# Sigmoid attention followed by a SiLU feed-forward on one core: batch 1's attention moved into the first matmul of batch 0, and the second matmul evened out to two pairs per batch

## Chip, cores, metric

One core of one Trainium2 chip. The metric is the device time of one execution in microseconds (us), median of several runs. The profiled span is 1.7 to 2.9 us shorter than that time, mostly 1.8, and all positions below are times from the start of the span.

Engine names: PE is the matrix engine (PEld its weight loads), DVE the vector engine, ACT the scalar engine with the sigmoids, POOL (GpSimd) casts and issues one DMA queue, SP issues the other.

## The reference

```python
# q, k, v: (8, 12, 448, 64), normal * 0.1
scores = q @ k.T / sqrt(64) - log(448)
attn   = sigmoid(scores)                # no softmax, so no row maximum and no row sum
x      = (attn @ v) -> (8*448, 768)
h      = x @ w_in                       # 768 -> 2048, "ff1" below
out    = (h * sigmoid(h)) @ w_out       # 2048 -> 768, "ff2" below
```

## The kernel before

Everything runs in float16 with float32 accumulation. A batch has 448 tokens. Its 12 heads are taken in three groups of four: groups 0, 1, 2 are batch 0, groups 3, 4, 5 are batch 1. The parts that matter:

```python
# loads: two queues
def load16(kind, i): ... nc.gpsimd.dma_start(...)        # POOL queue, casts to f16 on the way
def load32(kind, i): ... nc.sync.dma_start(st32[2 * (i % 2) + kind] ...)   # SP queue, stays f32
def cast(kind, i):   nc.gpsimd.tensor_copy(st16[i % 3][kind], st32[...])   # POOL
def dma_transpose(kind, i): nc.sync.dma_start_transpose(qkT[i % 3][kind], st16[i % 3][kind])
def pe_transpose(kind, i, pair): ...     # the same on PE with an identity, DVE copies PSUM to qkT

# attention: one score step = 4 small matmuls, then one sigmoid of 128x896 on ACT
def score_step(i, r, pair): ...          # needs qkT of group i
def value_steps(i, pair, rs): ...
def to_x(i, pair): ...                   # evicts attention output to xT

# [...]
dummy(14)                                # matmuls on zeros, to warm up PE
pe_transpose(1, 0, 0)
pe_transpose(0, 0, 1)
for n in range(NQ):                      # batch 0: 21 score steps, PE transposes of groups 1, 2 between
    for r in range(R):
        score_step(n, r, cnt % 2); sigmoid(n, r, cnt % 2)
        # [...] transposes, value_steps, or dummy(2)

for b in range(B):
    lo, hi = (b * S) // 256, ((b + 1) * S) // 256     # pairs of row blocks that batch b completes
    ff1(b, early)                        # 96 matmuls of 448 columns
    # ff2 of pairs lo..hi-1 (56 matmuls of 384 columns each, a Strassen-like form)
    # interleaved with the attention of batch b + 1
```

A pair is 256 tokens and a batch has 448, so batches 0 and 4 get one pair and the other six get two. q and k of the groups from 3 on come by SP as f32, are cast by POOL and transposed by DMA into qkT, the transposed q and k that the scores read; v comes by the POOL queue. The schedule rests on each engine taking its instructions in the order of the program. All four w_in pieces are queued in the opening, w_out right behind.

## Time and profile before

405.4 us (three runs, 404.7 to 405.8); the profiled execution took 406.5 us, with a span of 404.3 us. The total hides the structure, so I cut the span where each ff1 starts.

| stage (from ff1 of batch b to the next) | pairs of ff2 | us |
|---|---|---|
| start: attention of batch 0 | – | 34.4 |
| 0 | 1 | 49.8 |
| 1, 2, 3 | 2 each | 47.4 each |
| 4 | 1 | 40.4 |
| 5, 6 | 2 each | 47.3, 47.1 |
| 7 (no attention beside it) | 2 | 43.0 |

These come from the timeline of PE. A line gives start, length, engine, source line, operation, output<-inputs, form and count, and in brackets the idle time before it with what ended it. The 36-matmul runs are the halves of an ff1; those at 84.22, 131.66 and so on are the first halves:

```profile
63.91 0.59 PE L140 MATMUL att<-qkT,qkT 64*64 64x448 f16 x4 [7.20 <-DMA qkT<-st]
84.22 6.97 PE L215 MATMUL att<-xT,w_in_sb 128*128 128x448 f16 x36
131.66 6.97 PE L215 MATMUL att<-xT,w_in_sb 128*128 128x448 f16 x36
226.55 6.97 PE L215 MATMUL att<-xT,w_in_sb 128*128 128x448 f16 x36
266.92 6.97 PE L215 MATMUL att<-xT,w_in_sb 128*128 128x448 f16 x36
```

From 226.55 to 266.92 is stage 4. The line at 63.91 is a score of group 4 that waited 7.20 us for its DMA transpose; this happened behind ff1 of batch 0, in stage 0.

The busy time of the engines in three stretches (columns: stretch, length, then busy time and count of PE, PEld, DVE, ACT, POOL, then the granted PE clock, DMA share, GB/s): ff2 of stage 4, ff2 of a two-pair stage, and the score steps of batch 0:

```profile
244.00:266.90 22.90, 20.69 (x224) 10.03 (x223) 10.72 (x16) 19.52 (x23) 5.40 (x8) 1.00 0.57 102
286.00:314.00 28.00, 27.65 (x267) 13.90 (x266) 16.01 (x25) 19.46 (x21) 5.12 (x7) 1.00 0.55 111
8.00:34.40 26.40, 22.58 (x286) 9.55 (x286) 9.39 (x15) 19.45 (x21) 14.26 (x21) 1.00 1.23 209
```

In the two-pair stretch PE is busy 27.65 of 28.00 us: that stage is PE-bound. In the one-pair stretch PE has 20.69 of 22.90 and ACT 19.52: the 2 us of slack is what one-pair stages waste. The score steps of batch 0 run with the DMA engines at a share of 1.23 (above 1, so packets that overlap are counted more than once): busy throughout.

The score steps of batch 0, each four matmuls, with a dummy pair between (timeline of PE), and SP's queue, which shows when transposes are issued:

```profile
11.32 0.38 PE L140 MATMUL att<-qkT,qkT 64*64 64x448 f16 x4 [1.92 <-DVE qkT L127]
12.14 0.38 PE L140 MATMUL att<-qkT,qkT 64*64 64x448 f16 x4
12.46 0.61 PE L81 MATMUL ffp<-warm 128*128 128x512 f16 x2
```

```profile
28.24 2.76 SPq L110 DMA_TRANSPOSE qkT<-st  x2
31.06 5.98 SPq L101 DMA_DIRECT2D st<-in_k_dram  x2
53.48 6.26 SPq L110 DMA_TRANSPOSE qkT<-st  x2
```

A score step takes 0.38 us. Transposes of group 3 are issued at 28.24 and of group 4 at 53.48; the first score that needs group 3 comes at 50.8.

### The profile page before, as it was taken

The numbers are of one execution on the slowest core, as the hardware profiler recorded it, in microseconds if no ns is written. First come the engines' busy times: TensorE is split into PE (matmuls) and PEld (weight loads), VectorE is DVE, ScalarE is ACT, GpSimd is POOL, SyncE is SP. The second block draws the span as 40 slices with busy tenths as digits, with TensorE's granted clock in tenths as the row PEclk, the third lists the DMA queues.
The fourth block names the chain that finished last, engine by engine and source line by source line (L and its number), as shares of the span: only waits on it lengthen the run. The fifth ranks groups of instructions, "written<-read, shape, count | busy, mean of one in ns | idle before, by whom it ended". The sixth has DMA issues, their size and how long they took to land.

```text
span 404.3 us, 7303 instructions
## 1 busy us (share of the span) xinstructions
PE 378.2 (94%) x3026; PEld 188.3 (47%) x3026; DVE 201.6 (50%) x281; ACT 219.1 (54%) x251; POOL 81.5 (20%) x114
## 2 busy tenths in 40 slices
PE   6889956899999999999999998899999999999994
PEld 2334522455445545555455554455455544455452
DVE  1341545744646455544546354445645455544662
ACT  1885372924874348734677239933874348734200
POOL 7561034221222130022112022302112000000000
PEclk9999996999999999999999999999999999999999
DMA  8999987879977772767547783778178630311022
GB/s 194 199 206 200 208 151 155 161 156 214 161 150 159 180 148 47 175 133 178 107 72 188 175 172 71 155 162 163 39 143 164 170 47 2 78 42 40 0 78 78
DMA packets 69472, 53.78 MB, mean 133 GB/s; under 512 B 42304, under 2 KB 65856, under 8 KB 69440
## 3 DMA queue, kind: packets, MB, share of 16 engines
q1 hardware_dynamic: 55840, 40.38, 43.9%
q0 software_dynamic: 13600, 12.95, 21.8%
q8 instruction: 23, 0.38, 0.4%
q14 instruction: 9, 0.07, 0.1%
HBM read 45.61 MB, written 11.01 MB: 140 GB/s over the span
## 4 chain that ended last, share of the span: by engine, by line
PE 75%; DMA 12%; ACT 3%; POOL 3%; SPq 3%; issue 2%; DVE 1%; POOLq 0%; ACTq 0%
PE ffp L267 31%; PE att L215 24%; PE ffp L215 7%; PE att L156 7%; DMA st<-in_q_dram 7%; PE att L140 6%; DMA w_in_sb<-in_moe_w_in_dram 3%; ACT attnT L146 2%; SPq L101 2%; POOL st L104 1%; DMA st<-in_k_dram 1%; DMA qkT<-st 1%; ACT tsig L226 1%; SPq L110 1%; DVE gT L228 1%
## 5 line engine op out<-in xcount | busy, mean ns | idle before, releaser
L146 ACT ACTIVATE attnT<-att,bias_s 128x896 f16<-128x896 f32 x168 | 156.9, 1012 | 47.4 <-PE att L140 46.7
L215 PE MATMUL att<-xT,w_in_sb 128*128 128x448 f16 x576 | 111.8, 352 | 0.2 <-ACT xT L168 0.2
L215 PEld LDWEIGHTS <-w_in_sb 128*128 128x128 f16 x768 | 74.9, 98 | 70.6 <-issue 1.4
L230 ACT ACTIVATE tsig<-att 128x896 f16<-128x896 f32 x48 | 44.0, 917 | 99.6 <-PE att L215 99.6
L231 DVE TENSOR_TENSOR gT<-att,tsig 128x896 f16<-128x896 f32 x48 | 52.4, 1092 | 75.6 <-ACT tsig L230 75.6
L104 POOL CAST st<-st 128x896 f16<-128x896 f32 x42 | 40.7, 971 | 195.0 <-DMA st<-in_k_dram 153.4
L140 PE MATMUL att<-qkT,qkT 64*64 64x448 f16 x672 | 49.2, 360 | 12.5 <-DMA qkT<-st 8.0
L267 PEld LDWEIGHTS <-gs 128*128 128x128 f16 x448 | 40.0, 98 | 40.7 <-issue 12.0
L267 PE MATMUL ffp<-w_out_sb,gT 128*128 128x384 f16 x224 | 43.7, 328 | 3.4 <-DVE gT L228 3.4
L267 PEld LDWEIGHTS <-gT 128*128 128x128 f16 x336 | 31.1, 98 | 30.0 <-issue 11.6
L170 DVE TENSOR_SCALAR xT<-att 128x896 f16<-128x896 f32 x23 | 25.1, 1091 | 39.1 <-PE att L156 39.1
L267 PE MATMUL ffp<-wt,gs 128*128 128x384 f16 x224 | 42.5, 331 | 0.5 <-DVE gs L289 0.5
L267 PE MATMUL ffp<-w_out_sb,gs 128*128 128x384 f16 x224 | 42.4, 327 | 0.0
L215 PE MATMUL ffp<-xT,w_in_sb 128*128 128x448 f16 x192 | 39.0, 353 | 0.0
L278 DVE TENSOR_SCALAR snap<-ffp 128x384 f32<-128x384 f32 x42 | 23.4, 557 | 28.6 <-PE ffp L267 26.1
L156 PE MATMUL att<-attnT,v 64*64 64x448 f16 x672 | 37.5, 359 | 0.0
L97 POOL DMA_DIRECT2D v<-in_v_dram x48 | 28.6, 601 | 41.7 <-PE att L140 35.4
L140 PEld LDWEIGHTS <-qkT 64*64 64x64 f16 x672 | 17.8, 105 | 40.0 <-issue 32.4
L281 DVE SCALAR_TENSOR_TENSOR osb<-ffp,snap 128x384 f32<-128x384 f32 x42 | 23.3, 554 | 20.3 <-PE ffp L267 19.6
L156 PEld LDWEIGHTS <-v 64*64 64x64 f16 x672 | 18.4, 108 | 17.1 <-issue 8.8
L226 ACT ACTIVATE tsig<-ffp 128x448 f16<-128x448 f32 x32 | 17.2, 546 | 11.3 <-PE ffp L215 11.3
L228 DVE TENSOR_TENSOR gT<-ffp,tsig 128x448 f16<-128x448 f32 x32 | 19.7, 620 | 6.1 <-ACT tsig L226 6.1
(31 smaller groups left out, 126.4 us busy)
## 6 DMA issues: line engine op xcount, KB each, us to landing
out_dram<-osb SPq DMA_DIRECT2D x56, 192.0 KB, 2.8
st<-in_k_dram SPq DMA_DIRECT2D x44, 224.0 KB, 4.3
st<-in_q_dram SPq DMA_DIRECT2D x42, 224.0 KB, 4.9
v<-in_v_dram POOLq DMA_DIRECT2D x48, 112.0 KB, 4.1
w_in_sb<-in_moe_w_in_dram POOLq DMA_DIRECT2D x4, 768.0 KB, 10.9
w_out_sb<-in_moe_w_out_dram POOLq DMA_DIRECT2D x4, 768.0 KB, 22.8
st<-in_q_dram POOLq DMA_DIRECT2D x6, 112.0 KB, 7.5
qkT<-st SPq DMA_TRANSPOSE x42, 3.5
```

Of the source, the lines that this page charges most:

```text
L97: nc.gpsimd.dma_start(o[g * HP : (g + 1) * HP], src_of(kind, i, g))
L104: nc.gpsimd.tensor_copy(st16[i % 3][kind].rearrange("p r e d -> p e r d"), st32[2 * (i % 2) + kind].rearrange("p e (r d) -> p e r d", r=R),)
L140: nc.tensor.matmul(att[pair][cj, e, :S], kT[re, r, cj], qT[re, :, cj], start=True, stop=True)
L146: nc.scalar.activation(attnT[:, s0 : s0 + 2, :], att[pair][:, :, :S], AF.Sigmoid, bias=bias_s, scale=QKSCALE)
L156: nc.tensor.matmul(att[pair][e * HP : (e + 1) * HP, j, :S], vt[rj, e, r, :], attnT[rj, s0 + e, :], start=(r == 0), stop=(r == R - 1),)
L170: nc.vector.tensor_scalar_mul(xT[:, 2 * n : 2 * n + 2, :], att[pair][:, :, :S], SX)
L215: nc.tensor.matmul(o, w_in_sb[:, cc, f * P : (f + 1) * P], xT[:, cc, :], start=(cc == 0), stop=(cc == NCC - 1),)
L228: nc.vector.tensor_mul(gT[:, 2 * u + e, cb : cb + S], ffp[e][:, :S], ts[:, e])
L230: nc.scalar.activation(ts, ph[:, :, :S], AF.Sigmoid, bias=0.0, scale=ISX)
L231: nc.vector.tensor_mul(gT[:, 2 * u : 2 * u + 2, cb : cb + S], ph[:, :, :S], ts)
L267: nc.tensor.matmul(bank, a[:, fc], w[:, fc], start=first and fc == 0, stop=fc == KH - 1, skip_group_check=True,)
L278: nc.vector.tensor_scalar_mul(snap[i], bank, ISX)
```

## The change

Intent: no more one-pair stages. Attention of batch 1 runs inside ff1 of batch 0, where PE alone was busy and ACT idle; ff2 then runs two pairs per batch, one batch behind, for batches 1 to 7. The transposes in batch 0 are cut into halves and used as fillers between scores. Two w_in pieces and w_out are issued later, so that group 3 can come earlier. Two tiny memsets ("gates") keep SP from fetching groups 3 and 4 too early.

The core of the diff (definitions of the halved transposes and of ff1 as a generator cut):

```diff
-    xT = sb("xT", [P, NCC, S])
+    xT = [sb(f"xT{i}", [P, NCC, S]) for i in range(2)]
 [...]
     w_in_piece(1)
-    load16(2, 2)
-    w_in_piece(2)
-    w_in_piece(3)
-
-    dummy(14)
-    pe_transpose(1, 0, 0)
-    pe_transpose(0, 0, 1)
+    dummy(10)
+    for half in range(2):
+        pe_transpose(0, 0, 1, half, dve)
+    for half in range(2):
+        pe_transpose(1, 0, 0, half, act)
+    ff0 = ff1(0, (3, 2))
 [...]
+        (1, 0): [lambda: gate(3), lambda: fetch(3), T(1, 2, 0)],
 [...]
+        (1, 3): [T(0, 2, 1), lambda: prepare(3), lambda: w_in_piece(2)],
 [...]
+        (2, 0): [V(0, 6), X(0), lambda: gate(4), lambda: fetch(4)],
+        (2, 3): [V(1, 2, 3, 4), lambda: prepare(4), lambda: w_in_piece(3)],
+        (2, 6): [V(2, 0, 1, 2, 3), F("part", 0), V(2, 4, 5), F("part", 1)],
 [...]
+    us = units_of(1)                       # attention of batch 1, two steps at a time
+    visit(vs.pop(0))
+    for x in ff0:                          # between the column blocks of ff1 of batch 0
+        if vs and x[0] == "end" and x[1] % 4 != 1:
+            visit(vs.pop(0))
+    for s in range(4):
+        w_out_piece(s)
-    for b in range(B):
-        lo, hi = (b * S) // 256, ((b + 1) * S) // 256
+    for b in range(1, B):
 [...]
-            for m in range(lo, hi):
+            for m in (2 * b - 2, 2 * b - 1):
                 yield from ff2_pair(m)
```

`prepare(i)` is cast and DMA transpose of k and q of group i; `fetch(i)` is their loads and that of v.

## The prediction

> What bounds the kernel now. The page gives a span of 404.3 us, PE busy 94%; the chain of waits is 75% PE, 12% DMA. By stage (timeline of PE): batch 0's attention takes 34.4 us, paced by ACT (21 sigmoids of about 0.93 us) and by loads. Then each batch has ff1 (96 matmuls, 18.2 us) and ff2 mixed with the next attention. Stages with two ff2 pairs take 47.2 to 47.4 us and are PE-bound. Those with one pair are not: stage 4 takes 40.4 us (ACT sigmoids in its chain), stage 0 takes 49.8 us (8.0 us of PE waiting for DMA transposes, plus the one-time weight sums on DVE, eight of 0.95 to 1.68 us). The last stage takes 42.8 us. In the first 65 us the DMA is full.
>
> What the change does. Fourteen ff2 pairs remain, now two in each of batches 1 to 7. Batch 1's attention moves into ff1 of batch 0. Dummy matmuls become useful fillers. w_in pieces 2 and 3 move behind the casts of groups 3 and 4, w_out behind those of group 7.
>
> Cost. Before: 34.4 + 49.8 + 3x47.4 + 40.4 + 47.4 + 47.2 + 42.8. After: start + A + stage 1 + 5x47.2 + 42.8, where A is ff1 of batch 0 with attention of batch 1.
> Start: copies split over ACT and DVE save about 1 us, finer fillers about 1: 33 us.
> A: ACT needs 21x1.0 + 8 = 29 us, PE about 26, so ACT bounds it; plus 3.5 us for the last value product and its eviction: 33 us when data is there. It may not be: load, cast and transpose of one group recur every 10 us even without other traffic (transposes issued at 67.3, 77.1), and transposes beside weight loads are slow (issued 28.2, landed after 45). I expect about 6 us of waits for groups 4 and 5: A 39 us.
> Stage 1: 47 us plus about 4 for the weight sums, which load DVE beyond PE in the first pair. From the trace's rates (a weight piece 4 us, a group with transposes 10 us) all DMA work up to w_out's end adds to 95 to 98 us; the third product wants it at about 97. So little extra wait, but no slack: anything won earlier is lost there.
> Total: 33 + 39 + 51 + 236 + 43 = 402 us; without DMA waits 395 to 396. I say 400.5, range 393.5 to 408; chances: faster by over 2% 0.25, within 2% 0.70, slower 0.05.
>
> The Trainium skill ("DMA: Bandwidth & Descriptors", Queues, rings and completion order) says that each DMA engine goes round the queues packet by packet. The trace agrees: while w_out moved in 1536-byte packets, two transposes in 256-byte packets took about 15 us instead of 5.
>
> What would show it. Timeline: ff1 of batch 1 starting at about 72 us (not before 65), stages 2 to 6 at 47.2 us each including stage 4, last stage unchanged. In A, ACT nearly full except for waits of PE score matmuls for qkT of groups 4 and 5. In stage 1, DVE weight sums waiting for w_out or nearly, PE stalls of about 4 us in the first pair.
>
> What would make it wrong. Transposes landing in time: about 396. w_out landing past 100 us, or the clock falling to half in a PE stall as before at 55 to 61 us: 405 to 410. Score steps stalling behind k and q of group 2 in the start, because group 3's loads now compete earlier.

## The result, and the profile after

412.3 us (four runs, 410.6 to 412.8), against 405.6 us for the kernel before in four runs. Ratios in this document are the mean time of one kernel's runs over that of the other's of the same rounds, so not quite the ratio of the medians: here 1.0159, with an interval of 1.0122 to 1.0195. The change made the kernel 1.6% slower. That is within the 2% either way to which I had given a chance of 0.70, but above my range of 393.5 to 408 us.

The same lines of the timeline of PE for the changed kernel:

```profile
39.72 0.57 PE L137 MATMUL att<-qkT,qkT 64*64 64x448 f16 x8 [2.08 <-DMA qkT<-st]
54.50 0.59 PE L137 MATMUL att<-qkT,qkT 64*64 64x448 f16 x4 [6.64 <-DMA qkT<-st]
82.78 6.97 PE L217 MATMUL att<-xT,w_in_sb 128*128 128x448 f16 x36 [1.74 <-DVE xT L168]
131.66 6.97 PE L217 MATMUL att<-xT,w_in_sb 128*128 128x448 f16 x36
225.80 6.97 PE L217 MATMUL att<-xT,w_in_sb 128*128 128x448 f16 x36
272.86 6.97 PE L217 MATMUL att<-xT,w_in_sb 128*128 128x448 f16 x36
```

Read it by stages. "Stage A" is ff1 of batch 0 with the attention of batch 1; it begins with the first score of batch 1, at 39.72.

| | before | predicted | after |
|---|---|---|---|
| start (to the first score of batch 1) | – | 33 | 39.7 |
| stage A | – | 39 | 43.1 |
| sum: start of ff1 of batch 1 | 84.2 | 72 | 82.8 |
| stage 1 | 47.4 | 51 | 48.9 |
| stage 4 | 40.4 | 47.2 | 47.1 |
| stages 2, 3, 5, 6 | 189.3 | 188.8 | 188.4 |
| last stage | 43.0 | 42.8 | 43.1 |
| span | 404.3 | 402 | 410.2 |

So one ff2 pair left stage 0, and that brought ff1 of batch 1 forward by only 1.4 us. The pair was then paid for elsewhere: stage 4 grew by 6.7 us, the one-time weight sums moved into stage 1 (1.4 us). The deficit, 5.9 us, is the sum of these (-1.4 + 1.4 + 6.7) less the 0.9 us that stages 2, 3, 5 and 6 gained, plus 0.1 in the last. The later stages came out as predicted. The loss is in the first 83 us, where I was wrong by 10.8 us.

The score steps in the opening, SP's queue, and two stretches of busy time (5 us of the opening, and stage A):

```profile
11.31 0.59 PE L137 MATMUL att<-qkT,qkT 64*64 64x448 f16 x4 [0.57 <-ACT qkT L126]
12.39 0.59 PE L137 MATMUL att<-qkT,qkT 64*64 64x448 f16 x4
14.23 1.04 PE L81 MATMUL ffp<-warm 128*128 128x512 f16 x2
22.80 0.38 PE L137 MATMUL att<-qkT,qkT 64*64 64x448 f16 x4
27.54 0.64 PE L137 MATMUL att<-qkT,qkT 64*64 64x448 f16 x4
```

```profile
28.29 3.98 SPq L110 DMA_TRANSPOSE qkT<-st  x2
32.35 2.47 SPq L101 DMA_DIRECT2D st<-in_k_dram  x2
43.76 3.74 SPq L110 DMA_TRANSPOSE qkT<-st  x2
```

```profile
10.00:15.00 5.00, 3.95 (x34) 1.75 (x33) 1.25 (x2) 3.30 (x5) 1.71 (x3) 1.00 1.10 162
39.70:82.80 43.10, 32.38 (x257) 13.04 (x257) 12.08 (x15) 26.77 (x33) 13.67 (x18) 0.88 0.84 159
```

Three things are to be seen.

First, a score step takes 0.59 us until 22 us, then 0.38, and 0.64 again from 26.4 to 28.7 us. A dummy pair takes 1.04 instead of 0.61. By these lengths PE runs at about half clock for the first half of batch 0. The Trainium skill ("TensorE: Matmul & The Clock Gate", Part 1: The HAM clock gate) says that PE starts at half clock, and that a window of about 3.4 us of sustained work releases it. The traces agree only in part. The longer opening of the kernel before (14 dummies, 5.23 us) was followed by full-speed scores and the shorter one (10 dummies, 4.45 us) was not. But the number of dummies does not settle it: in runs 2, 4 and 14 below, also with 10, the eight transpose matmuls right behind them took 0.41 us, the full-speed length (0.64 here). In runs 2 and 4 the scores were at 0.59 us again from 10.5 and 11.7 us on; in run 14 they stayed at 0.38 until 19 us. The transposes of the opening, between which PE waits 0.8 and 0.7 us here, may count as well. Run 1 adds dummies in both places, so no run parts the two. Note that the stretch from 10 to 15 us shows a clock of 1.00 all the same; the matmul lengths are to be trusted there, not that column.

Second, the DMA transposes of group 3 are issued at 28.29, as late as in the kernel before (28.24), but now their scores come right behind: PE waits until 39.72. Group 4's are issued at 43.76 and land only by 54.50.

Third, ACT, which I had expected to be nearly full in stage A, is busy 26.77 of 43.10 us.

### The profile page after: what moved, and what is told of

The parts are those of the page before. It is cut to its first block, busy times and chain, and to the rows that moved or that the text cites. A ratio compares the mean times of both kernels' runs of the same rounds, so it can differ in the third digit from the quotient of the medians.

```text
span 410.2 us, 7255 instructions
## 1 busy us (share of the span) xinstructions
PE 382.4 (93%) x3000; PEld 188.6 (46%) x3000; DVE 198.5 (48%) x285; ACT 221.7 (54%) x255; POOL 81.4 (20%) x114
## 4 chain that ended last, share of the span: by engine, by line
PE 83%; DVE 5%; DMA 4%; ACT 4%; issue 2%; SPq 0%; POOL 0%; ACTq 0%; POOLq 0%
PE ffp L275 30%; PE att L217 25%; PE ffp L217 9%; PE att L137 8%; PE att L153 7%; DMA st<-in_q_dram 2%; ACT attnT L143 2%; DMA qkT<-st 2%; PE ffp L81 2%; PE att L119 1%; DVE qkT L126 1%; ACT tsig L233 1%; DVE gs L297 1%; DVE xT L168 1%; DVE wt L253 1%
## 5 line engine op out<-in xcount | busy, mean ns | idle before, releaser
L143 ACT ACTIVATE attnT<-att,bias_s 128x896 f16<-128x896 f32 x168 | 158.6, 1008 | 49.1 <-PE att L137 48.3
L217 PE MATMUL att<-xT,w_in_sb 128*128 128x448 f16 x552 | 109.2, 355 | 1.7 <-DVE xT L168 1.7
L237 ACT ACTIVATE tsig<-att 128x896 f16<-128x896 f32 x46 | 42.2, 917 | 92.7 <-PE att L217 92.7
L238 DVE TENSOR_TENSOR gT<-att,tsig 128x896 f16<-128x896 f32 x46 | 50.2, 1092 | 75.3 <-ACT tsig L237 75.3
L137 PE MATMUL att<-qkT,qkT 64*64 64x448 f16 x672 | 52.6, 379 | 12.2 <-DMA qkT<-st 8.7
L217 PE MATMUL ffp<-xT,w_in_sb 128*128 128x448 f16 x216 | 46.9, 364 | 0.0
L275 PE MATMUL ffp<-w_out_sb,gT 128*128 128x384 f16 x224 | 43.1, 327 | 0.4 <-DVE gT L235 0.4
L153 PE MATMUL att<-attnT,v 64*64 64x448 f16 x672 | 39.1, 360 | 0.3 <-DVE qkT L126 0.3
L137 PEld LDWEIGHTS <-qkT 64*64 64x64 f16 x672 | 18.7, 108 | 40.4 <-issue 33.9
L235 DVE TENSOR_TENSOR gT<-ffp,tsig 128x448 f16<-128x448 f32 x36 | 22.0, 620 | 26.1 <-ACT tsig L233 26.1
L233 ACT ACTIVATE tsig<-ffp 128x448 f16<-128x448 f32 x36 | 19.2, 548 | 11.3 <-PE ffp L217 11.3
```

What stands on the lines that cost most here:

```text
L137: nc.tensor.matmul(att[pair][cj, e, :S], kT[re, r, cj], qT[re, :, cj], start=True, stop=True)
L143: nc.scalar.activation(attnT[:, s0 : s0 + 2, :], att[pair][:, :, :S], AF.Sigmoid, bias=bias_s, scale=QKSCALE)
L153: nc.tensor.matmul(att[pair][e * HP : (e + 1) * HP, j, :S], vt[rj, e, r, :], attnT[rj, s0 + e, :], start=(r == 0), stop=(r == R - 1),)
L217: nc.tensor.matmul(o, w_in_sb[:, cc, f * P : (f + 1) * P], x[:, cc, :], start=(cc == 0), stop=(cc == NCC - 1), skip_group_check=split,)
L233: nc.scalar.activation(ts[:, e], ffp[e][:, :S], AF.Sigmoid, bias=0.0, scale=ISX)
L237: nc.scalar.activation(ts, att[pr][:, :, :S], AF.Sigmoid, bias=0.0, scale=ISX)
```

## The experiments

The theories:

- C: the cold clock costs the start.
- D: the start is bound by group 3's transposes, and the clock does not matter.
- G: the gates hold group 3 back.
- W: transposes are late because a w_in piece, issued right behind the casts, runs beside them.
- P: the chain load, cast, transpose is itself too slow, or DMA as a whole is full; then moving the weights only moves the wait.

Seventeen kernels ran, each timed beside the kernel before. In the table, "start" is the first score of batch 1, "waits" the waits of PE for qkT of groups 3, 4, 5, "ff1(1)" the start of ff1 of batch 1, all from the timeline of PE; the last columns are the median and the ratio to the kernel before.

| run | start | waits 3 / 4 / 5 | ff1(1) | us | ratio |
|---|---|---|---|---|---|
| changed kernel | 39.7 | 2.1 / 6.6 / 0 | 82.8 | 412.3 | 1.0159 |
| 1 warm | 36.4 | 3.2 / 5.8 / 0 | 79.5 | 410.0 | 1.0097 |
| 2 w_in early | 43.3 | 6.8 / 3.1 / 0 | 81.4 | 411.2 | 1.0111 |
| 3 warm and w_in early | 42.0 | 7.5 / 2.4 / 0 | 80.4 | 409.8 | 1.0099 |
| 4 no gates | 38.4 | 0 / 4.5 / 0 | 77.7 | 408.0 | 1.0045 |
| 5 warm, no gates | 37.7 | 3.2 / 5.8 / 0 | 79.3 | 408.6 | 1.0061 |
| 6 fourth w_in piece later | 37.4 | 3.9 / 2.7 / 4.4 | 80.7 | 409.8 | 1.0099 |
| 8 kernel before, 10 dummies | – | – | 86.9 | 407.5 | 1.0030 |
| 10 stale q, k (wrong) | 33.3 | 0 / 0 / 0 | 69.3 | 400.0 | 0.9814 |
| 11 half of w_in (wrong) | 34.6 | 0 / 3.6 / 0 | 72.8 | 401.2 | 0.9848 |
| 13 groups 3, 4 transposed on PE | 38.0 | 0 / 0 / 0 | 76.1 | 408.2 | 1.0064 |
| 14 the same, 10 dummies | 41.4 | 0 / 0 / 0 | 79.5 | 412.7 | 1.0157 |
| 15 ff1 first | 38.7 | 5.1 / 0.8 / 2.7 | 77.6 | 408.0 | 1.0047 |
| 16 ff1 first, w_in one group later | 34.3 | 0 / 0 / 4.7 | 76.4 | 407.4 | 1.0048 |
| 17 w_in one group later | 33.8 | 0 / 6.6 / 0 | 76.3 | 407.2 | 1.0007 |

Runs 7, 9 and 12 had mistakes of mine and are told below. The intervals of the ratios are about 0.005 to each side. Start, waits and ff1(1) are those of one profiled execution each. Nothing in which runs 5, 6 and 15 differ takes place before the first score of group 3, and yet they waited 3.2, 3.9 and 5.1 us there and started at 37.7, 37.4 and 38.7: differences of 1 to 2 us between single executions mean nothing.

### Runs 1 to 4: clock, weights, gates

Run 1, warm:

```diff
-    dummy(10)
+    dummy(14)
     for half in range(2):
         pe_transpose(0, 0, 1, half, dve)
+        dummy(2)
     for half in range(2):
         pe_transpose(1, 0, 0, half, act)
+        dummy(2)
```

> The changed kernel with 14 instead of 10 opening dummy matmuls and two more between each half of the opening transposes. Theory C (the start lost to a cold TensorE clock: four-matmul score steps of 0.59 us instead of 0.38 until 22 us): the score steps of batch 0 run at 0.38 us from the first on, the 21st sigmoid ends about 3 us earlier (about 33 us instead of 35.7), the load gate falls near 15.5 instead of 18.2 us, so group 3's transposes land about 2.5 us earlier and the total falls by 2 to 4 us, to 408 to 410 us. Rival D (the start is lost to the late transposes of group 3 alone): batch 0 ends earlier but PE waits longer for qkT, batch 1 still starts at 39.7 us, total unchanged at 412.

Timeline of PE in run 1:

```profile
12.01 0.38 PE L137 MATMUL att<-qkT,qkT 64*64 64x448 f16 x4
13.15 0.38 PE L137 MATMUL att<-qkT,qkT 64*64 64x448 f16 x4
36.38 0.96 PE L137 MATMUL att<-qkT,qkT 64*64 64x448 f16 x8 [3.20 <-DMA qkT<-st]
79.52 6.97 PE L217 MATMUL att<-xT,w_in_sb 128*128 128x448 f16 x36 [1.74 <-DVE xT L168]
```

The score steps are at 0.38 us, and ff1 of batch 1 starts 3.3 us earlier. The ratio falls from 1.0159 to 1.0097 (the two intervals overlap a little). C is right that the clock has a part, but D has one too: the sigmoids of batch 0 now end at 31.2 instead of 35.7, 4.5 us earlier, and PE stands 3.2 us for group 3. The gate memset sits in DVE's queue behind copies that wait for PE, so a warm PE also opens it earlier (at 16.4 instead of 18.2 us): group 3's transposes are issued at 24.3 instead of 28.3.

Run 2, all w_in pieces in the opening, as before:

```diff
+    w_in_piece(1)
     load16(2, 2)
-    w_in_piece(1)
+    w_in_piece(2)
+    w_in_piece(3)
 [...]
-        (1, 3): [T(0, 2, 1), lambda: prepare(3), lambda: w_in_piece(2)],
+        (1, 3): [T(0, 2, 1), lambda: prepare(3)],
-        (2, 3): [V(1, 2, 3, 4), lambda: prepare(4), lambda: w_in_piece(3)],
+        (2, 3): [V(1, 2, 3, 4), lambda: prepare(4)],
```

> The changed kernel with all four w_in pieces issued in the prologue, as the kernel before has it. Theory W (w_in pieces 2 and 3, issued right after the casts, run beside the transposes of groups 3 and 4 and delay them): transposes of group 3 take about 5 us from issue instead of 9 to 11, group 4 likewise, the 6.6 us wait shrinks to under 3 us, total 405 to 408 us. Rival P (the load, cast, transpose chain itself has a period of about 10 us, whatever the weights do): group 3's loads now land about 8 us later behind the weights, the start of batch 1 moves to 42 us or later, total unchanged or worse, 411 to 416.

Group 3 came 3.6 us later (start 43.3), group 4's wait halved to 3.1; total 411.2. The wait moved from group 4 to group 3, as P says. This run does not refute W: the pieces now ran beside group 3's loads and transposes.

Run 3, both edits:

> Both edits. If the two losses are independent the gains add (404 to 407 us). If the clock only moves the wait (D) it equals the early w_in alone; if the weights only displace the loads (P) it equals the warm one alone.

The result, 409.8, can be told neither from run 1 (410.0) nor, within noise, from run 2 (411.2); only the added gains of 404 to 407 us are ruled out. With the weights early, the warm opening changed the start by only 1.3 us: group 3 set it, with waits of 6.8 and 7.5 us.

Run 4, no gates: the two `gate(...)` calls are dropped.

> The changed kernel without the two memsets that hold back the fetches of groups 3 and 4. If the gate holds group 3 back too long (its k arrives at 27 us, the casts then wait 7.5 us for it), loads of group 3 land about 5 us earlier, its transposes by 33 us, and the total falls by 2 to 5 us. If instead early loads take bandwidth from groups 0 to 2, the first scores start later than 11.3 us and the total is the same or up to 3 us worse.

Group 3's transposes were issued at 21.0 us and landed at about 35.0 (39.6 in the changed kernel), before batch 0 was done, so its wait vanished; 408.0, ratio 1.0045. The score steps took 0.59 to 0.64 us here until 29 us, and yet this was better than run 1. G is right that the gates opened too late.

### Runs 5 to 8: combining, and two dead ends

Run 5, warm and no gates:

> The warm opening and no gates together. Alone they gave about 2 and 4 us. In the warm run batch 0 ended at 31.2 us and PE then waited 3.2 us for group 3; without the gates group 3 was there in time. If the clock and the gate are the two causes of the late start, batch 1 now starts at about 33 us without a wait. But group 4 landed at 50.3 us without gates, bound by DMA: then the wait for it grows from 4.5 to about 8 us and the total stays near 407. If group 4 follows group 3 forward, 404 us.

SP's queue and the timeline of PE:

```profile
20.79 2.95 SPq L110 DMA_TRANSPOSE qkT<-st  x2
37.68 0.57 PE L137 MATMUL att<-qkT,qkT 64*64 64x448 f16 x8 [3.16 <-DMA qkT<-st]
```

No gain on run 4 (408.6). Batch 0 was done early, but group 3, with transposes issued at 20.8, landed only for the score at 37.7: 17 us. Issuing them 7.5 us earlier than in the changed kernel brought them in only 2 us earlier. So what holds group 3 is mostly not when its transposes are issued; the next runs ask what runs beside them.

Run 6 adds, to run 5, the fourth w_in piece behind the casts of group 5 instead of group 4:

> As the last, and the fourth w_in piece moves from behind the casts of group 4 to behind those of group 5. Theory W (transposes of group 4 are slow because that piece runs beside them): they take 5 to 6 us from issue instead of about 10, the wait for group 4 falls by 4 to 5 us, total 402 to 404 us. Rival P (the chain itself is the limit): wait unchanged, total as the last or worse because the fourth piece arrives late for ff1.

Group 4's wait fell from 5.8 to 2.7 as W says, and group 5, which had none, got one of 4.4; total 409.8. The wait followed the weight piece.

Run 7 was meant to transpose groups 3 and 4 on PE:

> The changed kernel, warm, with groups 3 and 4 loaded and cast by the queue of GpSimd like groups 1 and 2 and transposed on TensorE (as batch 0 is), so that they need neither the cast nor the DMA transpose; group 5 is fetched early. If the chain load, cast, DMA transpose is what keeps batch 1 back, both waits of PE for qkT vanish, batch 1 starts at about 33 us, ff1 of batch 1 at 67 to 70 us, and the total is 395 to 399 us, below the kernel before. If stage A is slow for a reason of its own (PE and ACT alternating in order), it stays at 40 us or more and the total is 401 or above.

It gave a wrong result (relative error 0.2672) and 441.5 us. The loads of group 3 came ahead, in program order, of the opening transposes of group 0 that read the same buffer; PE waited 15.6 us for them. The wrong result itself has another source: run 9, without this mistake, shows the same error of 0.2672, from a misplaced load of v that run 7 has too. Nothing follows about the theories.

Run 8, the kernel before with `dummy(10)`:

> The kernel before with 10 instead of 14 opening dummy matmuls. If the number of dummies decides the clock in the start, its score steps take 0.59 us for some 10 us. There the start is also limited by ACT and by the loads, and group 3 is not needed until 51 us, so the total rises by at most 2 us, to 406 to 408; no change at all if the clock still comes up in time.

Its first scores take 0.59 us and ff1 of batch 1 comes at 86.9 instead of 84.2 us in the profiled run. In time it is 407.5, ratio 1.003 (0.998 to 1.008): within noise. The same cold opening costs the old order little that can be shown, since group 3 is not needed until 51 us.

### Runs 9 to 12: taking the waits away

Run 9, a second try at the PE transposes:

> The seventh run mended (there the loads of group 3 came ahead of the opening transposes in the program, so that those read group 3's rows): same idea, the loads of groups 3 and 4 now follow the transposes that free their buffers. Expectation as before: if the chain load, cast, DMA transpose keeps batch 1 back, no wait of PE for qkT of groups 3 and 4, batch 1 starts at about 33 us, stage A takes about 35 us, ff1 of batch 1 starts at 67 to 70 us, total 395 to 399 us. If stage A is slow for its own reason, 401 or above.

Wrong again, 430.0 us: v of group 5 was loaded, in program order, ahead of the value steps of group 1 that still read its buffer (PE waited 16.8 us).

Run 10: the warm kernel without cast and transpose of groups 3 to 5.

```diff
-        (1, 3): [T(0, 2, 1), lambda: prepare(3), lambda: w_in_piece(2)],
+        (1, 3): [T(0, 2, 1), lambda: w_in_piece(2)],
-        (2, 3): [V(1, 2, 3, 4), lambda: prepare(4), lambda: w_in_piece(3)],
+        (2, 3): [V(1, 2, 3, 4), lambda: w_in_piece(3)],
 [...]
-        at(("s", i, 3), lambda j=i + 2: prepare(j))
+        if i > NQ:
+            at(("s", i, 3), lambda j=i + 2: prepare(j))
```

> Wrong on purpose: the warm kernel without casts and DMA transposes of groups 3 to 5, so that the scores of batch 1 use the transposes of batch 0 and never wait for any. It shows start and stage A without that wait: batch 1 starts at about 32.5 us; stage A takes 33 us if ACT bounds it as predicted (29 us of ACT work and the end), or 36 to 37 us if the wait-free rest of stage A in the trace (43 less 6.6) is of another cause. Total 394 to 398 us.

Busy time of its stage A (same columns as above) and the start of ff1 of batch 1:

```profile
33.30:69.30 36.00, 30.46 (x260) 12.71 (x253) 12.70 (x16) 26.97 (x34) 10.23 (x14) 0.95 1.02 192
```

```profile
69.34 6.97 PE L217 MATMUL att<-xT,w_in_sb 128*128 128x448 f16 x36 [1.74 <-DVE xT L168]
```

400.0 us, ratio 0.9814. Without waits the start takes 33.3 us, as predicted, and stage A 36.0 instead of the 33 I had counted. ACT is still busy only 26.97 us of it: the waits of ACT for scores fall from 14.3 us in the changed kernel to 5.4, and the last 3.4 us of the stage are the last value product and its eviction. I put this down to PE and ACT taking turns in a fixed order, so that neither fills; no run changed that order with the waits gone. (With q and k of size 0.1 the sigmoid hardly depends on them, so the correctness check is blind to q and k. For every run here, the changed kernel too, "correct" does not vouch for q and k; only the order of the program does.)

Run 11: the warm kernel without w_in pieces 2 and 3.

```diff
-                            w_in_sb[:, cc, f * P : (f + 1) * P],
+                            w_in_sb[:, cc, f % 8 * P : (f % 8 + 1) * P],
```

> Wrong on purpose: the warm kernel without w_in pieces 2 and 3 (ff1 uses the first two pieces twice), so transposes of groups 3 and 4 run with no weight load beside them. Theory W: group 3 lands about 5 us after issue (by 30 us), no wait at the start of batch 1, wait for group 4 under 2 us, total 399 to 402. Rival P (the chain of load, cast, transpose, or loads slowed by other loads): the waits shrink by less than half, total 406 or above.

Timeline of PE and SP's queue:

```profile
45.30 0.38 PE L137 MATMUL att<-qkT,qkT 64*64 64x448 f16 x4 [3.58 <-DMA qkT<-st]
72.77 6.97 PE L217 MATMUL att<-xT,w_in_sb 128*128 128x448 f16 x36 [1.74 <-DVE xT L168]
```

```profile
27.69 3.76 SPq L110 DMA_TRANSPOSE qkT<-st  x2
37.92 3.28 SPq L110 DMA_TRANSPOSE qkT<-st  x2
47.72 3.23 SPq L110 DMA_TRANSPOSE qkT<-st  x2
```

401.2 us, and the wait for group 3 is gone although its transposes were issued 3.4 us later than in run 1. The later transpose of group 3 landed at most 4.3 us after its issue and that of group 4 after 5.2, against 9.1 and 8.0 in run 1. So two w_in pieces beside the transposes are most of the waits, which fall from 9.0 to 3.6 us in all (W). Group 4 still waited 3.6 us: transposes recur every 10 us even with no weight piece beside them, which is P, and I had expected less than 2.

Run 12, third try at the PE transposes:

> The ninth run mended: there v of group 5 was fetched, in program order, ahead of the value products of group 1 that still read its buffer, so PE waited 16.8 us for it and used the wrong v. Now it follows them. Expected: correct; no wait of PE for qkT of groups 3 and 4 since TensorE transposes them; batch 1 starts at 33 to 34 us; stage A takes 36 to 38 us, as the stale-scores run showed 36.0 us without any wait; ff1 of batch 1 starts at 70 to 72 us; total 398 to 402 us, faster than both kernels. If the loads of groups 3 and 4 or w_in pieces come too late because DMA itself is full, PE waits for them instead and the total is 404 or above.

425.0 us. Now the DMA transposes of group 5 came, in program order, ahead of the last scores of group 2 in the same buffer, and PE waited 18.6 us. Runs 7, 9 and 12 taught one lesson three times: in this kernel the order of the program, not the order in time, decides what waits for what.

### Runs 13 and 14: transposes on PE, warm and cold

The valid version of that idea. Groups 3 and 4 come by the casting queue and are transposed by PE, so that they need neither POOL's cast nor a DMA transpose:

```diff
+    load16(1, 3); load16(0, 3); w_in_piece(1); load16(2, 3)      # behind the opening transposes
 [...]
-        (0, 4): [T(0, 1, 1)],
+        (0, 4): [T(0, 1, 1), load16(1, 4), load16(0, 4), w_in_piece(2)],
+        (2, 1): [T(1, 3, 0), T(1, 3, 1)],
+        (2, 5): [T(0, 3, 0), T(0, 3, 1)],
 [...]                                   # group 4's in stage A; group 5 fetched from (2, 0) on
```

> The twelfth run mended: there the DMA transposes of group 5 came, in program order, ahead of the last two scores of group 2, whose buffer they overwrite, so PE waited 18.6 us for them. Now they follow batch 0. Expected if late transposes are the cause of the loss: no wait of PE for groups 3 and 4, batch 1 starts at 33 to 34 us, stage A takes 36 to 38 us, ff1 of batch 1 starts at 70 to 72 us, total 398 to 402 us. If the loads only move the wait elsewhere (DMA full), the total is 404 or above.

Timeline of PE around the inserted transposes of group 3:

```profile
30.02 0.38 PE L137 MATMUL att<-qkT,qkT 64*64 64x448 f16 x4
31.18 0.41 PE L119 MATMUL att<-ident,st 128*64 128x128 f16 x8 [0.78 <-DMA st<-in_q_dram]
32.38 0.36 PE L119 MATMUL att<-ident,st 128*64 128x128 f16 x6 [0.78 <-DVE qkT L126]
32.67 0.56 PE L137 MATMUL att<-qkT,qkT 64*64 64x448 f16 x4
```

No wait for qkT remains, and yet the start is at 38.0 and stage A takes 38.1; 408.2 us. From one score to the next took 2.65 us here instead of the usual 0.9: PE waits for the loads and for DVE's copies of what it has transposed. The waits were turned into round trips, and behind them PE ran at half clock for a while: the 16 value matmuls at 33.4 us took 1.71 us, 0.95 in run 1. My estimate of 398 to 402 was wrong.

Run 14 gives that kernel the cold opening:

> The same kernel with the changed kernel's opening (10 dummies, none between the opening transposes). It shows what the clock alone costs when no DMA transpose of group 3 stands behind it: if the cold clock costs time of its own, batch 1 starts 3 to 4 us later than in the run beside it and the total is 2 to 4 us higher; if the clock only mattered through the load gate, no difference beyond 1 us.

Timeline of PE in run 14:

```profile
9.93 0.38 PE L137 MATMUL att<-qkT,qkT 64*64 64x448 f16 x4 [0.57 <-ACT qkT L126]
18.01 0.41 PE L119 MATMUL att<-ident,st 128*64 128x128 f16 x8 [1.54 <-DMA st<-in_k_dram]
19.66 0.59 PE L137 MATMUL att<-qkT,qkT 64*64 64x448 f16 x4
```

412.7 against 408.2 us, ratios 1.0157 and 1.0064 with intervals of 0.004: the shorter opening costs about 4 us where no DMA transpose of group 3 stands behind it. It is not the clean test of a cold start that it was meant to be. In the profiled execution (410.2 us, the fastest of six) the scores begin at full length, and PE falls to half clock only at 19 us, behind a wait of 1.5 us for k of group 2; the granted clock from 20 to 25 us is 0.50, and 1.00 in run 13. The other five executions, of 411.4 to 413.6 us, left no trace. So a lower clock goes with the loss, but how much of the 4 us it makes is not shown. Beside runs 4 and 5, where the opening made no difference, this fits C and D together: the opening counts as far as group 3 is there in time.

### Runs 15 to 17: order of ff1, place of w_in

Run 15, on run 5: four column blocks of ff1 in a row ahead of group 4's first score.

```diff
-        if vs and x[0] == "end" and x[1] % 4 != 1:
+        if vs and x[0] == "end" and not 2 <= x[1] <= 5:
```

> The warm kernel without gates, with the attention steps of batch 1 moved within ff1 of batch 0: four column blocks of ff1 in a row ahead of the first score of group 4, where PE waited 5.8 us. If the in-order PE queue makes the wait for group 4 cost its full length although ff1 could have run, the wait falls to about 1 us, and since ACT still has its sigmoids left to do, stage A shrinks by about 3 us; total 404 to 406 us. If ACT bounds the rest anyway, total unchanged at 408.

Group 4's wait fell to 0.8, but group 5 now waited 2.7; 408.0, the same as run 5 within noise.

Run 16 has that order too, and each late w_in piece one group later, with the gate and fetch of group 3 at the second score of batch 0 and no gate for group 4:

```diff
-        (0, 1): [T(1, 1, 1)],
+        (0, 1): [T(1, 1, 1), lambda: gate(3), lambda: fetch(3)],
-        (1, 3): [T(0, 2, 1), lambda: prepare(3), lambda: w_in_piece(2)],
+        (1, 3): [T(0, 2, 1), lambda: prepare(3)],
-        (2, 3): [V(1, 2, 3, 4), lambda: prepare(4), lambda: w_in_piece(3)],
+        (2, 3): [V(1, 2, 3, 4), lambda: prepare(4), lambda: w_in_piece(2)],
 [...]                                   # w_in_piece(3) behind prepare(5)
```

> That order of steps, and each late w_in piece one group later (third behind the casts of group 4, fourth behind those of group 5), with group 3 fetched from the second score of batch 0 on. If the weights beside the transposes and the in-order waits are the two parts of the DMA loss: group 3 waits under 1 us, batch 1 starts at 33 to 34 us, group 4 waits under 2 us, stage A takes 37 us, total 400 to 403 us, below the kernel before. If DMA is simply full, the waits move to group 5 or to w_in and the total is 405 or above.

Run 17 is the same with the changed kernel's order of steps:

> As the last with the changed kernel's order of steps, to part the two. If the order alone brings the gain, this one stays at 405 to 408; if the weights' place alone, it is within 1 us of the run before it.

Timelines of PE in run 16 and in run 17:

```profile
34.25 0.55 PE L137 MATMUL att<-qkT,qkT 64*64 64x448 f16 x8
61.59 0.59 PE L137 MATMUL att<-qkT,qkT 64*64 64x448 f16 x4 [4.75 <-DMA qkT<-st]
76.43 6.97 PE L217 MATMUL att<-xT,w_in_sb 128*128 128x448 f16 x36 [1.54 <-DVE xT L168]
```

```profile
33.77 0.55 PE L137 MATMUL att<-qkT,qkT 64*64 64x448 f16 x8
47.75 0.59 PE L137 MATMUL att<-qkT,qkT 64*64 64x448 f16 x4 [6.65 <-DMA qkT<-st]
76.27 6.97 PE L217 MATMUL att<-xT,w_in_sb 128*128 128x448 f16 x36 [1.74 <-DVE xT L168]
```

Without the third w_in piece beside group 3's transposes (the second landed at about 27.5 us in both), batch 1 starts at 34 us without a wait in both. With the piece now beside group 4's, group 4 waits 6.65 us in run 17; with ff1 put there instead, group 5 waits 4.75 us in run 16. The starts of ff1 of batch 1 are within 0.2 us of each other. That is P in its second form: one wait for q and k of some group remains wherever the two pieces are put. Run 17, at 407.2 us and a ratio of 1.0007 (0.998 to 1.004), is even with the kernel before and has the lowest ratio of the valid versions, though run 4's interval overlaps; none beat the kernel before.

What stays open: whether some valid order could get the 400 us of run 10. That run leaves out six DMA transposes and run 11 leaves out 1.5 MB of f16 weights, so both also do less DMA work; they show the price of the waits, not that they can be avoided.

## Why the prediction was wrong, point by point

- **Right: the late stages.** Stages 2 to 6 were put at 47.2 us each and measured 47.1 to 47.2; the last was unchanged. Stage 4 went from 40.4 to 47.1 us.
- **Right by luck: w_out in time.** The third product started at 106.7 us, after a wait of 0.5 us for DVE's weight sum, and that sum started at 105.7. The last piece of w_out landed only at 105.0, not at 95 to 98, and past the 100 us that I had named as a danger. It did no harm because everything before it was late too. Stage 1 took 48.9 us, not 51: the DVE sums cost PE less than the 4 us estimated.
- **Right: waits in stage A for group 4.** "I expect about 6 us of waits for groups 4 and 5": 6.6 us, all for group 4 and none for group 5, so only the sum was right.
- **Wrong: "Start: copies split over ACT and DVE save about 1 us, finer fillers about 1: 33 us."** Measured 39.7. I costed the new opening with durations of a warm PE and did not ask whether 10 dummies still warm it. Run 1, with more dummies and score steps of 0.38 us, starts 3.3 us earlier. The rest is group 3: in the kernel before its transposes had until 51 us, and I counted waits for groups 4 and 5 but none for group 3. Run 10, warm and without waits, starts at 33.3, 3.1 us before run 1.
- **Wrong in size: "ACT bounds it; plus 3.5 us [...]: 33 us when data is there."** Run 10 measured 36.0. The sum of ACT's work was nearly right (26.97 us busy, to my 29) and so was the end (3.4 us), but ACT also waited 5.4 us for PE's scores, and those waits were missing from the sum. That the fixed order of PE and ACT makes them is my reading, not tested.
- **Wrong: "without DMA waits 395 to 396".** Run 10 shows 400.0 (span 398.2), for the reason of the last point.
- **The headline.** My own sum was 402, and I quoted 400.5, leaning on luck. Neither allowed for the 2 us or so by which the device time exceeds the span (1.8 in the profiled execution).

The sum of the first 83 us: predicted 72; 0.3 more in the start without waits, 3.1 group 3, 3.3 what run 1's opening wins back, 3.0 stage A's own length, 0.6 more wait for group 4, and 0.4 left over (PE ran at half clock behind that wait until 60 us; what that cost was not measured). That makes 82.7, measured 82.8. The split between clock and group 3 holds for this order of the edits only: with the gates gone, the same opening moved the start by 0.7 us (runs 4 and 5).

Of my list of what would make it wrong, "the clock falling to half in a PE stall" was near: I had looked for it in a stall, not in the opening. And the warning that "anything won earlier is lost there" was right in kind but in the wrong place. DMA was the limit for q, k and w_in of batch 1, not for w_out.

The Trainium skill ("DMA: Bandwidth & Descriptors", Queues, rings and completion order), as cited in the prediction, has each DMA engine go round the queues packet by packet. The kernel before shows it from 34 to 44 us, with w_out in the POOL queue (q0) and transposes in SP's (q1). The columns are packets, MB, and the share of the time of 16 engines (DMA view):

```profile
q0 software_dynamic: 1154, 1.71, 93.9%
q1 hardware_dynamic: 1157, 0.29, 22.1%
```

The two queues moved packets one for one, though not bytes. The experiments agree with what follows from it: removing the traffic of the late w_in pieces brought group 3's transposes in without a wait (run 11), and postponing it by a group did the same (runs 16 and 17).

## What to carry to other kernels

Work that moves ahead of something it used to hide behind brings its loads forward too; ask which transfers lose their slack, and what runs on the DMA engines beside them. When moving one transfer out of the way moves the wait to the next consumer, as in runs 2, 6, 15, 16 and 17, suspect that the queue is full; no reordering tried here helped. Warm-up matmuls are part of the schedule: check after each change of the opening that the first real matmuls run at their warm length, by the length of the matmuls and not by the clock column.

## What the Trainium skill lacked or had wrong

- "TensorE: Matmul & The Clock Gate" gives about 3.4 us of sustained work as what releases the clock, and does not say how busy is busy enough. In the changed kernel PE was busy 3.95 of the 5 us from 10 to 15 and 4.45 us with its dummies before that, and its score steps stayed at 0.59 us until 22 us; with the same 10 dummies run 14 had score steps of 0.38 us until 19 us.
- The same page warns that clock events can be unreliable. It does not say that a granted clock of 1.00 may stand beside matmuls of half-clock length: so from 10 to 15 us in the changed kernel, while dummy pairs took 1.04 us instead of 0.61.
- "DMA: Bandwidth & Descriptors" says that queues share an engine by packets, but has no figure for a DMA transpose beside casting loads. Here the later of two transposes landed 15.3 us after its issue with two w_in pieces beside it (run 5), and 7.2 us after it with only the end of one (run 17).
- No page says that a transfer placed too early in the program can make PE wait for data that it would only need later; runs 7, 9 and 12 waited 15.6, 16.8 and 18.6 us for such loads or transposes.
